# Projections and feed-forward: the form of the matmuls chosen group by group, in a new order of instructions

## The chip, the cores and the metric

The program runs on one core of a Trainium2 chip. The metric is the device time of one execution in microseconds; of the kernel before there are three, from 1133.86 to 1136.08, with a median of 1133.97. TensorE appears in the profile as PE (matmuls) and PEld (loads of weights into the array), VectorE as DVE, ScalarE as ACT, GpSimd as POOL, and SyncE, which only starts DMAs, as SP.

## The reference

One block of a transformer with modulation. x has 2048 tokens of width 1024; 32 heads of width 32 share one key and value head; the feed-forward width is 3584. All in bf16.

```
mod = (silu(c) @ w_mod) as six rows: sa, ca, ga, sb, cb, gb
h = layernorm(x) * (1 + ca) + sa
q = h @ wq  (32 heads of 32);  k = h @ wk;  v = h @ wv   (one head)
p = softmax(q k^T / sqrt(32));  o = p v
x = x + ga * (o @ wo)
h = layernorm(x) * (1 + cb) + sb
x = x + gb * ((silu(h @ w1) * (h @ w3)) @ w2)
```

## The kernel before

**Tiling.** Queries go in 8 blocks of 256 tokens (n = 0 to 7), a block in 8 units of 4 heads (f), a unit in 8 steps of 256 keys (j). That makes 512 score steps. One step (`s_exp`) is 8 matmuls of 32 rows, four heads side by side in the array, into four PSUM banks out of the six of tile S6, and two exponentials of 128x1024 on ACT, which write U. The banks form three slots of two; the scores of an exponential wait until the one three before it has read its slot. U is summed in pairs on DVE (PS) and multiplied by V in a column form (`av_mm`, 128x32, four heads beside each other), and the row sums come from products of PS with ONES, also in columns.

**What fills TensorE between score steps.** While ACT works through the exponentials of one block, PE does other products: the q projections (`q_proj`), the output projection of an earlier block (`wo`), its first feed-forward products (`slab`, 14 for a block: 256 columns of w1 and of w3, then a tanh on ACT and two products on DVE), and its second ones (`quarter`, 4 for a block: 28 products for each of two tiles of tokens). In the last block nothing is left for ACT after the last exponential, and the rest of `wo`, `slab` and `quarter` follows on PE alone. The weights of a slab (W13, 512 KB for each of w1 and w3) go round in few buffers, those of a quarter (W2S, 1792 KB) in two; SP starts each load when the last reader of its buffer is done. In the profile and the lists of instructions the feed-forward weights are called W or HT and W2S (some lie in buffers that had other names), the second norm's output and the queries both QT, the gated product HT.

**Two forms.** A product of 128x128 weights can be one matmul (the full form), or four of 128x32 weights, one for each 32 columns of the array (the column form). The `av` products are of the column form anyway. `prods` (lines 890 to 899) writes both versions; `mode_of` (line 533) chooses. For a node with a column version:

```
return n.col[1][0] or ("C" if self.mode in ("A", "C") and self.ncol < self.COLS and self.load < self.FULL else "F")
```

`self.mode` is the form of the matmul before on PE (A stands for av, C for columns, F for full, S for scores), `ncol` counts column nodes since the last av, and `load` is a running count that grows with dense instructions. A node is a group of two products. `n.col[1]` is a list `form` with one entry; in `q_proj`, `wo` and `slab` four nodes, which add up in one bank, share one list, so the first of the four decides for all. The nodes of `quarter` have no column version.

**The order.** Every instruction is a node of a graph (class `Graph`); class `Placer` places nodes on engines. `ORDER` is a long string of node numbers (with a "b" where the second engine that could do it is taken), and the nodes are issued in that order. Each engine works off its own list strictly in order, waiting on semaphores where a node needs another's result. All instructions are issued in line 22 (`play`), so the profile names no other line. A second program with a guard against overflow stands behind a branch and is not executed here.

Of the kernel before, what the change touches and what calls it, by code (L numbers as in the profile page):

```python
# [8 lines left out]
P = 128  # L9
# [110 lines left out]
6 1 11 0 4 2 5 8 3 7 9 12 13 10 25 16-18 59 22 15 14 60 19 61 28 21 62 412 63 27 20 23 64 24 65 26 29 68 30 31 36 45  # L120
37 32 66 33 38 69 39 40 103 67 34 102 41 35 70 104 131 105 71 123 42 72 132 73 122 106 74 43 124 112 107 46 125 44
133 75 126 47 48 134 108 49 135 50 76 136 111 109 127 113 77 137 128b 114 110b 115 129 116 130 117b 78 118 79 80 119
99 172 81 82 171 97 55b 54 53 51 85 58 98b 57 52b 56 173 163 83 86b 174 162 175 138 84 164 182 87 176 139 88 165 89
143 90 166 91 92 142 167 93 94 168 95 183 140 96 144 460 152 145 141b 120 146 151 461 169 153 147 121 462 154 148b
463 155 170b 464 149 156 184 242 185 157b 150 186 177b 421 191 465 187 158 243 192 178 159 193 188b 466 194 179b 195
467 160 202 196 468 197b 469 180 161 470 203 198 181 471 204 472 199b 205 189 473 206 211 100 190b 207 474 475 101
208b 227 477 228 212 229 230 200 476 231 213 244 214 209 215 201b 245 478 246 210 216 232 233 247 234 235 217b 479
222 236 223 248 224 225 480 218 249 226 481 219 250 252 253 251 254 255 487 482 257-260 483 256 501 261 220 502 485
237 503 504 221 238 488 239 505 240 262 263 506 241 484 507 491-493 489 494 508 264 265 509 495 510 266 496 497 511
486 498 499 267 268 512 500 513 490 269 514 270 526 307 515 516 308 517 271 309 310 525 518 519 272 520 311 273 274  # L130
528 521 522 275 523 527 302 303 524 276 562 304 563 305 529-531 564 565 306 532 533 566 541 538 539 567 277 540 568
542 534 543 569 535-537 544 278 570 548 571 553 545 572 546 552 279 547 280 573 549 574 550 297 281 575 298 551 299
# [4 lines left out]
640 646-648 661 649 652 650 662 357 663 680 358 359 664 651 665 360 681 666 327 361 328 667 653 668 654 332 669 333  # L137
682 334 670 335 655 671 336 329 672 330 683 322 673 331 674 323 675 684 324 325 676 677 326 337 678 338 685 413 679
703 414 430 339 418 704 417 415 340 416 686 688 705 706 689 690 707 687 691-693 341 694 708 695 709 699 696 710 697
# [8 lines left out]
834 835 930 836 931 1313 840 1314 828 837 1315 457 411 838 1316 839 1317 458 841 1318 842 843 846-848 1319 459 1320  # L148
# [3 lines left out]
911-913 1369 1335 914 915 1370 916 1336 917 918 890 1383 919 972 891 892 1371 1372 893 920 894 895 1373 896 1340 897  # L152
921 951 922 1338 898 1375 1374 923 899 924-926 1341 1376 927 928 900 1342 973 901 1377 902 1378 1386 903 904 1379
905 906 929 907 1380 952 1406 908 1351 1408 1381 932-934 1407 935 936 1352 937 938 1387 939 1392 940 993 1354 1393
1384 1409 1394 1355 1410 1395 1396 941 1397 1398 1411 1399 1356 1412 1388 942 1413 943-945 1402 946 1414 947 1389
1415 948 1382 949 1416 953 1390 994 954-956 1417 950 1418 957 1385 958 1419 959 960 844 1432 963 1014 964 961 965
1421 1420 966 962 967 968 1433 969 1422 970 974 1391 1015 975 976 1423 971 1424 977 978 845 1425 979 1435 980 981
984 982 1035 985 1427 1426 1436 986 987 983 988 989 1428 990 991 995 992 1036 996 1429 997 1455 1400 1456 998 1401
999 1000 1430 1001 1457 1002 1016 1056 1017 1458 1437 1003 1018 1019 1459 1020-1022 1004 1023 1460 1461 1431 1077
1441 1442 1024 1403 1443 1434 1444 1462 1445 1025 1446-1448 1404 1463 1464 1438 1005 1006 1465 1007 1405 1008 1439  # L160
1009 1010 1466 1011 1451 1467 1440 1012 1468 1026 1481 1057 1027-1030 1469 1470 1013 1031 1032 1471 1482 1033 1037
1078 1038 1034 1039 1472 1040 1473 1041 1474 1042 1484 1043 1044 1047 1045 1098 1048 1476 1475 1485 1049-1051 1046
1052 1477 1053 1054 1058 1055 1099 1059 1478 1060 1504 1449 1505 1061 1450 1062 1063 1479 1064 1506 1065 1507 1119
1490 1452 1491 1066 1492 1453 1493 1508 1494 1067 1495 1496 1454 1497 1509 1510 1500 1068 1486 1069 1511 1070-1073
1512 1074 1487 1513 1075 1488 1514 1079 1120 1080 1081 1076 1082 1083 1515 1480 1516 1084 1085 1517 1483 1086 1089
1140 1090 1489 1091 1087 1092 1519 1518 1088 1093-1095 1530 1520 1096 1100 1141 1101 1102 1521 1103 1097 1522 1104
1531 1105 1523 1106 1107 1533 1110 1161 1111 1108 1525 1524 1112 1109 1113-1115 1534 1526 1116 1117 1121 1118 1162
1122 1527 1123 1553 1498 1124 1554 1499 1125-1127 1501 1128 1555 1502 1556 1738 1503 1539 1540 1129 1528 1541 1542
1557 1543-1545 1130 1546 1558 1559 1549 1131 1529 1132 1560 1133 1134 1532 1135 1136 1561 1535 1562 1137 1138 1563
1142 1739 1143 1139 1144 1145 1564 1536 1565 1146 1147 1537 1566 1148 1149 1579 1152 1759 1153 1150 1154 1155 1567  # L170
1568 1151 1156 1157 1538 1158 1569 1159 1163 1160 1760 1164 1165 1570 1571 1580 1547 1166 1572 1548 1167-1169 1550
1170 1551 1573 1574 1780 1552 1173 1174 1577 1171 1175 1176 1575 1177-1179 1172 1180 1576 1781 1600 1181 1183 1184
1601 1578 1185-1187 1583 1188 1602 1603 1585 1586 1604 1581 1587-1590 1605 1606 1582 1591 1592 1607 1189 1596 1190
1584 1191 1192 1608 1609 1593 1594 1610 1193 1595 1194-1196 1611 1597 1598 1612 1197 1624 1198 1613 1199-1202 1614
1599 1615 1625 1203 1204 1616 1626 1205-1208 1617 1209 1618 1627 1210 1619 1214 1211 1244 1215-1217 1620 1212 1621
1628 1218 1219 1622 1220-1223 1629 1623 1647 1224 1225 1648 1226 1630 1227 1632 1633 1649 1650 1631 1634 1635 1651
1636-1639 1652 1653 1643 1228 1229 1654 1230 1231 1640 1641 1655 1671 1656 1232 1233 1657 1234 1235 1672 1236 1237
# [229 lines left out]
7223 7264-7270 7273 7271 7274-7276 7272 7277 7289 7278-7288 7290  # L407
# [1271 lines left out]
```

## Time and profile before

| | us |
|---|---|
| median of three executions | 1133.97 |
| the profiled execution's span | 1132.8 |
| start to the first exponential | 30.95 |
| first to the end of the last exponential | 1001.55 |
| end of the last exponential to the end | 100.30 |

The profiled execution's own span is 1132.8; some 1.2 us of the median lie outside it. The profile page gives busy times of each engine. A row of the groups names the engine, the operation, the tile written and those read, the shape and the count, then busy time and mean duration of one, then the idle time ahead of them and what ended it. A row of the timeline has the start, the time to the end of the last of the instructions merged into it, and in brackets the idle time ahead of it with what it waited for. "128*32" behind a matmul is the size of its weights in the array; in the lists of instructions the same reads "32x256", that is 32 columns out and 256 wide. A matmul's own duration (273 ns) is longer than its share of PE's time, since matmuls overlap; the time from start to start counts.

### The profile page before, as it was taken

The numbers are of one execution on the slowest core, as the hardware profiler recorded it, in microseconds if no ns is written. First come the engines' busy times: TensorE is split into PE (matmuls) and PEld (weight loads), VectorE is DVE, ScalarE is ACT, GpSimd is POOL, SyncE is SP. The second block draws the span as 40 slices with busy tenths as digits, with TensorE's granted clock in tenths as the row PEclk, the third lists the DMA queues.
The fourth block names the chain that finished last, engine by engine and source line by source line (L and its number), as shares of the span: only waits on it lengthen the run. The fifth ranks groups of instructions, "written<-read, shape, count | busy, mean of one in ns | idle before, by whom it ended". The sixth has DMA issues, their size and how long they took to land.

```text
span 1132.8 us, 36935 instructions
## 1 busy us (share of the span) xinstructions
PE 1104.8 (98%) x16642; PEld 754.1 (67%) x16642; DVE 983.7 (87%) x1615; ACT 1021.8 (90%) x1160; POOL 41.0 (4%) x92
## 2 busy tenths in 40 slices
PE   6999999999999999999999999999999999999998
PEld 5744546766567766777577766776567756776887
DVE  7998999897889889998999899998999999997442
ACT  5999999999999999999999999999999999994110
POOL 4300000000000000000000000000000010000000
PEclk9999999999999999999999999999999999999999
DMA  9321487664476675965496577868597557777893
GB/s 345 108 76 32 155 217 202 197 191 110 123 224 196 174 195 150 247 193 154 122 290 197 144 190 193 236 196 217 141 253 215 160 148 194 219 204 196 235 240 105
DMA packets 379429, 209.16 MB, mean 185 GB/s; under 512 B 15488, under 2 KB 371072, under 8 KB 379264
## 3 DMA queue, kind: packets, MB, share of 16 engines
q1 hardware_dynamic: 378832, 206.59, 65.8%
q8 instruction: 132, 2.16, 0.8%
q14 instruction: 33, 0.27, 0.1%
q10 hardware_dynamic: 432, 0.13, 0.0%
HBM read 199.89 MB, written 4.19 MB: 180 GB/s over the span
## 4 chain that ended last, share of the span: by engine, by line
ACT 46%; PE 43%; DVE 6%; DMA 3%; issue 1%; SPq 1%; POOL 0%; DVEq 0%
ACT U L22 44%; PE PB L22 31%; PE S L22 13%; ACT HT L22 3%; DVE PS L22 2%; DMA W<-in_A_wq_dram 1%; DVE ST L22 1%; DMA W2S<-in_B_w_dram 1%; DVE HT L22 1%; SPq L22 1%; DMA W<-in_B_w_dram 1%; DVE X L22 0%; POOL RS L22 0%; DVE QT L22 0%; DVE RB L22 0%
## 5 line engine op out<-in xcount | busy, mean ns | idle before, releaser
L22 ACT ACTIVATE U<-S 128x1024 bf16<-128x1024 f32 x1024 | 967.5, 1143 | 5.3 <-PE S L22 3.9
L22 DVE TENSOR_TENSOR PS<-U 128x2048 bf16<-128x2048 bf16 x256 | 309.1, 1213 | 16.6 <-ACT U L22 14.8
L22 DVE TENSOR_TENSOR PS<-PS 128x1024 bf16<-128x1024 bf16 (+1 forms) x401 | 272.4, 690 | 4.2
L22 PE MATMUL PB<-QT,W 128*128 128x256 bf16 (+1 forms) x2448 | 228.4, 273 | 0.6 <-DVE QT L22 0.5
L22 PE MATMUL S<-QT,KT 32*128 32x256 bf16 x4096 | 203.7, 273 | 7.4 <-ACT U L22 4.7
L22 PEld LDWEIGHTS PB<-QT,W 128*128 128x128 bf16 (+1 forms) x2448 | 169.3, 97 | 43.5 <-issue 22.8
L22 PE MATMUL PB<-W2S,HT 128*128 128x256 bf16 x1512 | 190.2, 273 | 0.0
L22 PEld LDWEIGHTS PB<-W2S,HT 128*128 128x128 bf16 x1512 | 136.9, 98 | 42.2 <-issue 24.0
L22 PEld LDWEIGHTS S<-QT,KT 32*128 32x128 bf16 x4096 | 60.9, 92 | 135.2 <-ACT U L22 115.3
L22 PE MATMUL PB<-U,V 128*32 128x256 bf16 x4096 | 128.7, 273 | 0.6 <-ACT U L22 0.5
L22 PE MATMUL PB<-QT,HT 128*128 128x256 bf16 (+1 forms) x1248 | 116.5, 273 | 1.2 <-issue 1.1
L22 PEld LDWEIGHTS PB<-U,V 128*32 128x32 bf16 x4096 | 101.4, 96 | 23.1 <-issue 13.3
L22 PE MATMUL PB<-HT,W 128*32 128x512 bf16 (+2 forms) x800 | 100.0, 338 | 0.9 <-DVE HT L22 0.9
L22 PEld LDWEIGHTS PB<-QT,HT 128*128 128x128 bf16 (+1 forms) x1248 | 85.1, 97 | 22.0 <-issue 11.7
L22 ACT ACTIVATE HT<-PB 128x512 bf16<-128x512 f32 (+1 forms) x106 | 79.5, 750 | 3.6 <-PE PB L22 3.4
L22 DVE SCALAR_TENSOR_TENSOR HT<-HT,PB 128x512 bf16<-128x512 bf16 x99 | 67.6, 683 | 7.4 <-ACT HT L22 6.3
L22 DVE TENSOR_TENSOR HT<-HT,PB 128x512 bf16<-128x512 bf16 x100 | 68.2, 683 | 5.5 <-PE PB L22 4.4
L22 PEld LDWEIGHTS PB<-HT,W 128*128 128x128 bf16 (+1 forms) x800 | 50.1, 97 | 32.9 <-issue 11.5
L22 ACT ACTIVATE HT<-S 128x512 bf16<-128x512 f32 (+1 forms) x17 | 11.8, 696 | 61.6 <-PE S L22 61.6
L22 PE MATMUL PB<-WO,QT 128*128 128x512 bf16 x224 | 55.7, 381 | 0.0
L22 DVE STREAM_TRANSPOSE RB<-PB 128x256 f32<-128x256 f32 x63 | 28.0, 445 | 25.6 <-PE PB L22 25.5
L22 POOL TENSOR_SCALAR RS<-MV 128x1 f32<-128x1 f32 x32 | 12.3, 387 | 1002.3 <-DVE MV L22 774.8
(119 smaller groups left out, 680.9 us busy)
## 6 DMA issues: line engine op xcount, KB each, us to landing
W<-in_B_w_dram SPq DMA_DIRECT2D x150, 512.0 KB, 4.9
W2S<-in_B_w_dram SPq DMA_DIRECT2D x30, 1792.0 KB, 8.4
HT<-in_B_w_dram SPq DMA_DIRECT2D x74, 512.0 KB, 4.8
W2S<-in_w_mod_dram SPq DMA_DIRECT2D x8, 1024.0 KB, 6.4
X<-in_A_x_dram SPq DMA_DIRECT2D x8, 512.0 KB, 6.7
U<-in_w_mod_dram SPq DMA_DIRECT2D x4, 1024.0 KB, 12.1
out_dram<-X SPq DMA_DIRECT2D x7, 512.0 KB, 8.2
W2S<-in_A_x_dram SPq DMA_DIRECT2D x5, 512.0 KB, 12.2
```

The costliest lines, as they stand in the source:

```text
L22: return getattr(e, call[0])(*call[1], **call[2])
```

## The change

Four edits of the code and a new table.

- In `q_proj`, `wo` and `slab` each node has its own list `[None]` in place of the shared `form`. Each group of two products takes the form that PE's state suggests when its turn comes, and one bank can be summed in both forms.
- In `quarter` the nodes are built with `prods` and so have a column version.
- The full version passes skip_group_check=True, as the column version did.
- `SWITCH`, the placer's cost for a change of form, is 0.096 and 0.121 for F and S, where it was 0.095 and 0.11.
- `ORDER` is another order of the same nodes.

```diff
 ORDER = """
-6 1 11 0 4 2 5 8 3 7 9 12 13 10 25 16-18 59 22 15 14 60 19 61 28 21 62 412 63 27 20 23 64 24 65 26 29 68 30 31 36 45
...
+11 6 7 5 8 12 9 13 10 16-18 22 15 14 19 21 20 60 59 69 61 68 23 27-29 70 112 24 102 111 113 26 37 36 103 104 123 122
...
 """
...
-    SWITCH = {"F": 0.095, "S": 0.11, "A": 0.106, "C": 0.106}
+    SWITCH = {"F": 0.096, "S": 0.121, "A": 0.106, "C": 0.106}
...
     def prods(lst):
         def full(b=None):
-            return [lambda e, o=o, w=w, x=x, st=st, sp=sp: e.matmul(o(b, 0, P), w(0, P), x(), start=st, stop=sp)
+            return [lambda e, o=o, w=w, x=x, st=st, sp=sp: e.matmul(o(b, 0, P), w(0, P), x(), start=st, stop=sp, skip_group_check=True)
                     for o, w, x, st, sp in lst]
...
             for m in range(2):
                 for sub in range(2):
-                    form = [None]
                     for c0 in range(0, NC, 2):
...
-                           vt=vt + 0.01 * m, mode="F", sess=ss[m], post=0.145, col=(cols, form))
+                           vt=vt + 0.01 * m, mode="F", sess=ss[m], post=0.145, col=(cols, [None]))
...
                 for f0 in range(0, NF, 2):
-                    op("pe", lambda b, t=t, f0=f0: [lambda e, f=f: e.matmul(
-                        BANK[b][:, t * B:(t + 1) * B], HHT[:, f, t * P:(t + 1) * P], w2[:, f, :], start=(f == 0),
-                        stop=(f == NF - 1)) for f in range(f0, f0 + 2)], pe_mm(B, 2),
-                       reads=[key] + [("HHT", x) for x in range(f0 // 2, (f0 + 1) // 2 + 1)],
-                       writes=[("f2", n, q, t), ("f2", n, q)], vt=vt, mode="F", sess=s, post=0.145)
+                    full, cols = prods([(
+                        lambda b, y, z, t=t: BANK[b][y:z, t * B:(t + 1) * B],
+                        lambda y, z, t=t, f=f: HHT[:, f, t * P + y:t * P + z],
+                        lambda f=f: w2[:, f, :], f == 0, f == NF - 1) for f in range(f0, f0 + 2)])
+                    op("pe", full, pe_mm(B, 2), reads=[key] + [("HHT", x) for x in range(f0 // 2, (f0 + 1) // 2 + 1)],
+                       writes=[("f2", n, q, t), ("f2", n, q)], vt=vt, mode="F", sess=s, post=0.145, col=(cols, [None]))
```

The edit of `form` in `q_proj` and `wo` reads as in `slab`. What the new order does is seen in the lists of instructions. Three places of PE's list follow; `S<-QT,KT` is a score step, `PB<-QT,W` and `PB<-QT,HT` are slab products, `PB<-W2S,HT` quarter products, `PB<-U,V` av products, and `PS,ONES` the row sums.

Near the end of the third block's scores, at 382 us of the profile. Before:

```order
L22 MATMUL PB<-QT,HT 128x256 x14
L22 MATMUL S<-QT,KT 128x256 x8
L22 MATMUL PB<-QT,HT 128x256 x8
L22 MATMUL PB<-QT,W 128x256 x8
L22 MATMUL S<-QT,KT 128x256 x8
L22 MATMUL PB<-PS,ONES 32x256 x4
L22 MATMUL PB<-QT,W 32x256 x96
L22 MATMUL S<-QT,KT 128x256 x8
L22 MATMUL PB<-W2S,HT 128x256 x12
```

Of the change:

```order
L22 MATMUL PB<-QT,HT 128x256 x4
L22 MATMUL PB<-QT,W 128x256 x8
L22 MATMUL S<-QT,KT 128x256 x8
L22 MATMUL PB<-PS,ONES 32x256 x4
L22 MATMUL PB<-QT,W 32x256 x64
L22 MATMUL S<-QT,KT 128x256 x8
L22 MATMUL PB<-QT,W 128x256 x8
L22 MATMUL PB<-W2S,HT 128x256 x4
L22 MATMUL S<-QT,KT 128x256 x8
L22 MATMUL PB<-W2S,HT 128x256 x14
L22 MATMUL S<-QT,KT 128x256 x8
```

The slab products that stood in one run of 96 column matmuls between two score steps stand on both sides of a score step now, 64 in columns and 8 in full form.

The end of the loop, the last two score steps and what comes behind them. Before:

```order
L22 MATMUL PB<-W2S,HT 128x256 x22
L22 MATMUL S<-QT,KT 128x256 x8
L22 MATMUL PB<-W2S,HT 128x256 x12
L22 MATMUL S<-QT,KT 128x256 x8
L22 MATMUL PB<-W2S,HT 128x256 x22
L22 MATMUL PB<-U,V 32x256 x64
L22 MATMUL S<-W2S,HT 128x256 x12
```

Of the change:

```order
L22 MATMUL PB<-W2S,HT 128x256 x12
L22 MATMUL S<-QT,KT 128x256 x8
L22 MATMUL PB<-W2S,HT 128x256 x14
L22 MATMUL S<-QT,KT 128x256 x8
L22 MATMUL PB<-W2S,HT 128x256 x28
L22 MATMUL S<-U,V 32x256 x8
L22 MATMUL PB<-W2S,HT 32x256 x16
L22 MATMUL S<-U,V 32x256 x8
L22 MATMUL PB<-W2S,HT 32x256 x16
L22 MATMUL S<-U,V 32x256 x48
```

The step of 22 products ahead of the second but last score step has 12; behind the last score step stand more quarter products, some of them in columns between the av products.

The slabs of the last block, behind the last exponential. Before:

```order
L22 MATMUL S<-QT,W 128x256 x16
L22 MATMUL S<-QT,HT 128x256 x16
L22 MATMUL PB<-QT,W 128x256 x2
L22 MATMUL S<-QT,W 128x256 x12
L22 MATMUL PB<-QT,W 128x256 x6
L22 MATMUL S<-QT,W 128x256 x16
L22 MATMUL PB<-QT,W 128x256 x4
```

Of the change:

```order
L22 MATMUL S<-QT,W 128x256 x36
L22 MATMUL PB<-QT,W 128x256 x2
L22 MATMUL S<-QT,HT 128x256 x2
L22 MATMUL PB<-QT,W 128x256 x4
L22 MATMUL S<-QT,HT 128x256 x4
L22 MATMUL PB<-QT,W 128x256 x6
L22 MATMUL S<-QT,HT 128x256 x2
L22 MATMUL PB<-QT,W 128x256 x2
L22 MATMUL S<-QT,HT 128x256 x10
```

Before, a buffer of weights is mostly read by 16 matmuls in a row; now the groups of two that use different buffers alternate, so the last reader of a buffer comes later and the next load into it starts later.

More of the change, by code (lines that the diff above doesn't have):

```diff
@@ new lines @@
+1739 1780 1244 1620 1624 1595 1626 1211 1597 1628 1621 1214 1215 1622 1216-1219 1647 1623 1648 1649 1220-1222
+1632-1634 1650 1635 1636 1223 1637 1224 1651 1652 1638 1653 1225 1639 1226-1228 1598 1627 1630 1625 1212 1631 1599
+1643 1629 1654 1656 1640 1229 1641 1230-1232 1655 1642 1644 1645 1657-1659 1245 1246 1233-1235 1247 1660-1664
+1248-1251 1236-1238 1665 1252-1256 1239 1666 1668 1257 1258 1667 1669 1670 1240 1259 1260 1241 2158 1261 2159 1673
+1671 1675 1646 1672 1676 1242 1677 1674 1678 2160 1262 1263 1679-1681 2161 1682 1264 1683 1684 2162 1685 1265 2164
@@ new lines @@
+2063 1823 1822 1843 1790 2301 2303 2304 2291 2292 2278 1305 1791 2248 2249 2295 2281 2282 1803 1804 2305 1805
+1792-1795 2306 2307 1796 2308 1806 1797-1799 1807 2309 2283 2284 1800 2310 1808 1809 2311 1810 1813 1814 2312 1811
+2313 2325 1812 1815-1818 2314 1819 1820 2315 1824-1826 1821 2316 1827 2317 2293 1828 1829 2318 1830 2294 1831
+1834-1837 2320 1838 1832 2319 1844 1885 1864 1865 2296 2328 1833 2321 1839-1841 1845 1846 2348 1847 1848 2323 1842
+2329 2322 2349 2350 1849-1851 2334 1852 2351 2335 2336 1853 2337 2352 2338-2340 2353 2341 2354-2356 2297 2326 2330
@@ new lines @@
+2000 2008 2460 2472 2001 2431 2462 2009 2013 2014 2010 2015 2463 2016 2464 2440 2017 2465 2018 2441 2019-2021
+2023-2026 2467 2027-2030 2475 2022 2473 2476 2443 2470 2031 2033 2466 2468 2034 2495 2035 2036 2469 2496 2497
+2037-2041 2498 2481 2042 2482 2043 2483 2484 2499-2501 2485 2502 2486 2044 2487 2045 2488 2504 2046-2050 2503 2477
+2471 2474 2478 2444 2479 2445 2480 2491 2505 2506 2051 2507 2489 2052-2055 2508 2490 2056 2057 2510 2064 2065
+2058-2060 2066 2509 2521 2061 2631 2094 2511-2513 2067-2071 2514 2072 2073 2516 2074-2076 2515 2077 2517 2078 2079
@@ new lines @@
+3288-3290 3305 2829 3291 3306 3292 3277 3250 3251 2830 3293-3295 2831 3308 3307 3278 3252 3298 3284 3281 3285 3309
+3310 2832-2837 3311 2842-2845 2838 2846 3312 2839 3286 3313 2847 3314 2848 2849 2852 2853 3315 2850 3328 2851
+2854-2857 3317 2858 3316 3318 3319 2859 2863 2864 3287 2860 2865 2866 3320 3296 2867 2868 3329 3297 2869 2870 3321
+2871 2873-2876 3323 2877-2880 3326 2872 3327 3299 3331 2881 2883 3322 3324 3325 2884 3351 2885 2886 3352 3353
+2887-2891 3354 3337-3340 2892 3341 3355-3357 2893 3358 2894-2898 3360 3342 3343 2899 3344 2900 2901 3359 3300 3333
@@ new lines @@
+4410-4412 4893 4862 4413 4918 4414 4406 4426 4427 4448 4468 4447 4415 4919 4902-4905 4920 4906 4891 4864 4416 4907
+4921 4908 4909 4417 4922 4923 4865 4894 4866 4912 4892 4924 4418-4423 4925 4428 4424 4429-4432 4895 4425 4898
+4926-4928 4438 4433-4435 4929 4436 4439-4443 4931 4899 4437 4930 4932 4933 4444 4445 4449-4452 4934 4453 4935 4942
+4446 4897 4900 4943 4454-4456 4459-4461 4937 4462 4463 4457 4458 4901 4936 4938 4464-4466 4470 4471 4467 4945 4489
+3006 4510 4469 4490 4472 4965 4910 4473-4475 4939 4966 4967 4911 4476 4477 4968 4951 4952 4478 4953 4954 4969
@@ new lines @@
+4955-4957 4970 4958 4971 4940 4913 4256 4479 4914 4941 4915 4961 4946-4948 4491 4492 4972 4973 4493-4496 4974 4480
+4481 4497 4498 4482 4975 4499 4500 4483-4486 4977 4487 4501-4504 4944 4949 4488 4950 4976 4978 4979 4505 4980
+4506-4508 4512-4514 4981 4509 4982 4983 4959 4515-4517 4960 4991 4962 4518 4531 4511 4552 3007 4553 4532 4984 4519
+4522-4524 4986 4525 4526 4985 4520 4987 4527-4529 4988 4963 4521 4964 4530 4989 4992 4994 4533 5014 4534 5015
+4535-4540 5017 5000-5002 5016 4541 5003 5018 5004 5005 4542 5019 5006 5007 5020 5021 4543-4548 5023 4549 5022 4550
@@ new lines @@
+5149 5148 5151 5669 5155 5150 5153 5154 5681 4714 4715 5682 5158-5160 4716 5654 5649 5651 5161 5162 5683 5684
+5163-5166 5685 5179 5180 5686 5181 5167 5182-5184 5687 5185 5186 5189 5688 5190 5187 5191 5689 5192 5193 5690 5656
+4717 5652 5188 5194 5195 5691-5693 5196 5168-5173 5694 5174 5695 5175 5657 5699 5197 5658 5700 5176 5200 5696
+5201-5203 5722 5667 5204 5205 5668 5723 5206 5207 5708-5710 5725 5711 5724 5208 5219 5240 5220 5261 5241 5450 5726
+5712 5713 5670 5697 5671 5209 5714 5715 5727 5210 5728 5729 5698 5672 5718 5702 5211-5216 5731 5221 5217 5222-5225
@@ new lines @@
+6210 6192 6193 6685 6194 6195 6211 6656 6196 6686 6197 6687 6198 6212-6214 6688 6657 6199 6658 6689 6215-6217
+6690-6692 6218 6219 6223-6226 6693 6227 6220 6228 6694 6229 6230 6233 6231 6695 6659 5968 6660 6701 6232 6702
+6234-6236 6696 6237 6238 6697 6239 6240 6244-6246 6724 6241 6704 6698 6669 6247-6249 6725 6726 6670 6250 6251 6727
+6710 6711 6243 6263 4719 6284 6285 6264 6336 6252 6712 6713 6728 6714 6699 6672 6253 6715-6717 6265 6730 6266 6729
+6731 6732 6673 6674 6720 6700 6706 6707 6267-6272 6254 6733 6255 6273 6256 6734 6274 6257 6258 6735 6259-6261 6736
@@ new lines @@
+7120-7124 7115 7116 7125 7104-7108 6427 7117 7141 7142 7126 7143 7127 7144 7145 7130-7132 7146 7133 7134 7147 7148
+7135 7151 7152 7136 7137 7153-7158 7149 7128 7192 7129 6428 7150 7138 7159 7161-7182 7193 7183 7184 7194 7185 7195
+7196 7186 7187 7197-7199 7188 7200-7202 7189 7190 7203 7225 7204 7226 7205 7206 7227 7228 7207 7229-7235 7208
+7236-7240 7209 7241 7210 7211 7242 7212-7214 7243 7244 7215-7222 7257-7261 7245 7246 7262 7263 7247 7264-7267 7248
+7268-7270 7249 7250 7273-7275 7251 7252 7276-7286 7271 7253 7254 7272 7287 7288 7191 6429 7223 7255 7289 7290
@@ L1138, in q_proj @@
                 op("pe", full, pe_mm(w, 2) * cold, reads=wk + hk, writes=[("q", n, f)], vt=vt, mode="F", sess=s, post=0.145,
-                   col=(cols, form))
+                   col=(cols, [None]))
             op("dve", lambda b: [lambda e: e.tensor_scalar(
@@ L1386, in wo @@
                     s = Sess()
-                    form = [None]
                     for q in range(4):
@@ L1395, in wo @@
                            reads=[(k, *i) for f in range(2 * q, 2 * q + 2) for k, i in (("QT", (n, f)), ("WOG", (f,)))],
-                           writes=[("wo", n, t, h)], vt=vt, mode="F", sess=s, post=0.145, col=(cols, form))
+                           writes=[("wo", n, t, h)], vt=vt, mode="F", sess=s, post=0.145, col=(cols, [None]))
                     xs = X1[:, n % NX, t, h * 512:(h + 1) * 512]
@@ L1462, in slab @@
                 for sub in range(2):
-                    form = [None]
                     for c0 in range(0, NC, 2):
```

464 lines of the change are left out of this document (220 added, 244 removed), and 43 rows, old and new, of the table ORDER.

## The prediction

> **What bounds the kernel now.** I read the page's busy shares first, then the windows, cut at the first and the last exponential, then the timeline of ScalarE and TensorE at the places where ScalarE stands idle.
>
> ```profile
> span 1132.8 us, 36935 instructions
> PE 1104.8 (98%) x16642; PEld 754.1 (67%) x16642; DVE 983.7 (87%) x1615; ACT 1021.8 (90%) x1160; POOL 41.0 (4%) x92
> ...
> 0.00:30.95 30.95, 19.73 (x287) 16.79 (x288) 23.50 (x59) 18.07 (x20) 14.72 (x43) 1.00 0.99 346
> 30.95:1032.50 1001.55, 988.67 (x15454) 654.99 (x15453) 917.95 (x1479) 995.40 (x1128) 24.47 (x46) 1.00 0.65 178
> 1032.50:1132.80 100.30, 96.39 (x906) 82.33 (x903) 42.27 (x78) 8.38 (x15) 1.76 (x4) 1.00 0.76 202
> ```
>
> The columns of the last three rows are the stretch, its length, the busy time of PE, weight loads, DVE, ACT and POOL, the granted clock and the DMA share. There are three parts: 30.95 us of startup, a body of 1001.55 us in which ACT is busy for 995.40, and a tail of 100.30 us in which only PE is full. The clock is 1.00 in all three, so it plays no part.
>
> In the body ACT sets the end: it has only 1001.55 - 995.40 = 6.15 us of idle time. PE is nearly as full, but waits for ACT to free the banks of the scores:
>
> ```profile
> PEld S L22 <- ACT U L22: 115.3, 413, 1.1
> ...
> ACT U L22 <- PE S L22: 3.9, 9, 0.9
> ...
> 54.02 112.61 ACT L22 ACTIVATE U<-S 128x1024 bf16<-128x1024 f32 x122 [0.40 <-PE PB L22]
> ...
> 385.92 0.72 ACT L22 ACTIVATE HT<-PB 128x512 bf16<-128x512 f32 x1
> 386.42 1.15 ACT L22 ACTIVATE U<-S 128x1024 bf16<-128x1024 f32 x1
> 388.10 4.69 ACT L22 ACTIVATE U<-S 128x1024 bf16<-128x1024 f32 x5 [0.54 <-PE S L22]
> ```
>
> 122 exponentials took 112.61 us, or 0.92 each; a tanh pushes the next one back by 386.42 - 385.92 = 0.50. One score step feeds two exponentials, so PE has 1.84 us from step to step, 2.34 with a tanh. The last row shows a break: ACT stood for 0.54 us because a score step came late; the waits (first two rows: total, times, longest) count nine such, 3.9 us together. What PE did ahead of it:
>
> ```profile
> 384.38 0.40 PE L22 MATMUL S<-QT,KT 32*128 32x256 bf16 x8
> 384.70 0.29 PE L22 MATMUL PB<-PS,ONES 128*32 128x256 bf16 x4
> 384.82 2.79 PE L22 MATMUL PB<-QT,W 128*32 128x256 bf16 x96
> 387.55 0.51 PE L22 MATMUL S<-QT,KT 32*128 32x256 bf16 x8
> ```
>
> The step took 387.55 - 384.38 = 3.17 us, 0.83 over 2.34. PE's lead over ACT took 0.29 of that and ACT lost 0.54. I call "unit" one product of 128x128 by 128x256, either one matmul in the full form or four in the column form. This step holds 24 + 1 units and 2 for the scores; 27 units in 3.17 us, less two changes of form, leave 0.109 us a unit if a change costs 0.11.
>
> **The change part by part.** What the form itself costs:
>
> ```profile
> 54.14 1.04 PE L22 MATMUL PB<-HT,W 128*128 128x512 bf16 x4
> 55.11 0.40 PE L22 MATMUL S<-QT,KT 32*128 32x256 bf16 x8
> ...
> 56.34 1.04 PE L22 MATMUL PB<-HT,W 128*32 128x512 bf16 x16
> 57.30 0.40 PE L22 MATMUL S<-QT,KT 32*128 32x256 bf16 x8
> ...
> L22 PEld LDWEIGHTS PB<-QT,W 128*128 128x128 bf16 x1584 | 144.3, 98 | 41.7 <-issue 21.7 <-DVE QT L22 1.4 <-DVE PS L22 0.4
> L22 PEld LDWEIGHTS PB<-QT,W 128*32 128x32 bf16 x832 | 21.8, 97 | 1.4 <-issue 1.1
> ```
>
> Eight units took 55.11 - 54.14 = 0.97 us in full form and 57.30 - 56.34 = 0.96 in columns, each with one change behind it. So the form is free; only the change of form costs. The 1579 matmuls more (counted in the two built programs: 16642 and 18221) are whole units turned into four pieces, and weigh nothing by these rows. The Trainium skill, "TensorEngine Tiling (Array Packing)", section Restrictions, speaks against that: column tiling switches Fast Weight Load off. The rows above do not bear it out as a loss here: 97 against 98 ns a load, and the same step time. By that rule the sum below would only grow.
>
> *Changes of form.* Counted in the two instruction lists they fall from 1109 to 1059; 50 x 0.11 = 5.5 us less work for PE, all in the body. This by itself gains nothing, since ACT ends the body; it counts only where a step overruns.
>
> *Body.* With 0.109 a unit and 0.1 a change I added up each of the 511 stretches from score step to score step in both lists. Before, 201 exceed ACT's 1.84 (2.34), by 50.6 us together; after, 174 by 32.6. The deepest are gone: four steps of 27 units (the one at 384.38 and its three like in other blocks) and one of 24 near the end:
>
> ```profile
> 513.01 1.94 ACT L22 ACTIVATE U<-S 128x1024 bf16<-128x1024 f32 x2 [0.51 <-PE S L22]
> ...
> 763.64 1.94 ACT L22 ACTIVATE U<-S 128x1024 bf16<-128x1024 f32 x2 [0.50 <-PE S L22]
> ...
> 889.03 1.94 ACT L22 ACTIVATE U<-S 128x1024 bf16<-128x1024 f32 x2 [0.47 <-PE S L22]
> ...
> 1028.74 3.77 ACT L22 ACTIVATE U<-S 128x1024 bf16<-128x1024 f32 x4 [0.90 <-PE S L22]
> ...
> 1025.79 2.57 PE L22 MATMUL PB<-W2S,HT 128*128 128x256 bf16 x22
> 1028.30 0.40 PE L22 MATMUL S<-QT,KT 32*128 32x256 bf16 x8
> ```
>
> In the new order the same place holds 64 column matmuls, a score step, then the rest in full form: 16 + 1 + 2 units and two changes, 2.3 us, within 2.34. The idle time that goes is 0.54 + 0.51 + 0.50 + 0.47 + 0.90 = 2.92 us; a break also costs up to 0.22 more, because an exponential alone takes 1.15 (row 386.42) and one in a row 0.92. Five breaks are worth 2.92 to 4.0; I take 3.5. Against it, three new steps exceed by about 0.71 (26 units with a tanh): 0.71 - 0.29 = 0.42 each, +1.3 (bounds 0 and +1.9). The shallow overruns that are left shrink by a third, from 46.3 us to 30.5. Of ACT's idle time 3.9 - 2.92 = 0.98 us is put down to them by name, at most 6.15 - 2.92 = 3.23 with all that names nothing: -0.3 to -1.1, and I take -0.7. Body: -3.5 + 1.3 - 0.7 = **-2.9** (bounds -4.0 - 1.1 = -5.1 and -2.9 + 1.9 = -1.0).
>
> *Tail, work.* Behind the last score step PE has 895 units before and 909 after (the instruction lists): 14 x 0.109 = **+1.5**. This is the price of the relief in the body: what no longer overruns there is done later, where nothing hides it.
>
> *Tail, loads.* PE waited for two loads before:
>
> ```profile
> 1030.04 0.40 PE L22 MATMUL S<-QT,KT 32*128 32x256 bf16 x8
> ...
> 1035.39 1.48 PE L22 MATMUL S<-W2S,HT 128*128 128x256 bf16 x12 [0.58 <-DMA W2S<-in_B_w_dram]
> ...
> 1082.18 1.48 PE L22 MATMUL S<-QT,W 128*128 128x256 bf16 x12 [0.48 <-DMA W<-in_B_w_dram]
> ...
> W<-in_B_w_dram SPq DMA_DIRECT2D x150, 512.0 KB, 4.9
> W2S<-in_B_w_dram SPq DMA_DIRECT2D x30, 1792.0 KB, 8.4
> ```
>
> A weight buffer is loaded again when its last reader has ended. From there to the first matmul that reads the new contents I counted units of PE. Before, the shortest distance in the tail was 5.7 us (the second wait: 5.7 + 0.48 = 6.2 needed), the others 6.5 or more. After, five buffers have 4.8, 4.8, 5.0, 5.0 and 5.0, four more 5.4 to 5.9. The median landing is 4.9, the one late load 6.2: I take 5.3, which waits 2 x 0.5 + 3 x 0.3 = 1.9. For W2S the distance grows from 8.6 (0.58 short, so 9.2 needed) to 9.6: 0.3 for the queue. Sum 2.2 against 0.58 + 0.48 = 1.06: **+1.1** (bounds: at 4.9, 0.2 - 1.06 = -0.9; at 5.7, 4.4 + 0.8 - 1.06 = +4.1).
>
> *Startup.* The first exponential hangs on eight scalings of the first wq columns and on the projection behind them:
>
> ```profile
> 24.37 1.71 DVE L22 TENSOR_SCALAR WO<-W,MODC 128x256 bf16<-128x256 bf16 x6 [0.40 <-DMA W<-in_A_wq_dram]
> ...
> 24.43 2.03 POOL L22 TENSOR_SCALAR WO<-W,MODC 128x256 bf16<-128x256 bf16 x2 [1.10 <-DMA W<-in_A_wq_dram]
> ...
> 27.46 1.05 PE L22 MATMUL PB<-HT,WO 128*128 128x256 bf16 x8 [0.84 <-POOL RS L22]
> ...
> 28.63 1.91 PE L22 MATMUL PB<-HT,WO 128*128 128x256 bf16 x16
> 30.47 0.40 PE L22 MATMUL S<-QT,KT 32*128 32x256 bf16 x8
> ```
>
> In the new lists POOL does three of them, up to 24.43 + 3 x 1.0 = 27.5, about when PE's first bank came free before, and the 24 matmuls run with no warm-up products among them: 2.6 us in place of 3.0, of which a later start takes part. I take -0.1, with 0.5 either way (half a scaling on POOL). SP's queue holds the same bytes ahead of wq. The end of the program, two DVE operations and the last output, is as it was: nothing.
>
> *Sum:* -0.1 - 2.9 + 1.5 + 1.1 = -0.4. The profiled span of 1132.8 becomes 1132.4. The median of the runs, 1133.97, is 1.2 above that span, so the median should be 1133.6.
>
> **The rivals.**
>
> *Faster: the body wins and the loads arrive.* Body -4.6, near its lower bound, and tail waits as before: -0.1 - 4.6 + 1.5 + 0 = -3.2, 1130.8. For it: 413 waits of PE on ACT mean that PE has room in most steps. Against it: the tail must have +1.5, and distances of 4.8 leave nothing.
>
> *Slower: the tail's loads.* Place: PE's slab matmuls behind the last score step. If a 512 KB load needs 5.7 us from release to landing there, as the one at 1082.18 needed more, the loads cost +4.1 and with a body of -2.0 the sum is -0.1 - 2.0 + 1.5 + 4.1 = +3.5, 1137.5. With the body at -2.9 the loads turn the sign from +1.5 on (a landing of about 5.4) and can be told from no change from +3.8 on (about 5.65). For it: DMA is busy at 0.76 of the tail and a wait pushes only PE. Against: before, all but one of the loads came in time.
>
> *Slower: PE runs out of instructions.* PE stood still twice in the body with no semaphore named, 1.1 us together:
>
> ```profile
> PE PB L22 <- issue: 1.1, 2, 0.9
> ...
> q8 instruction: 132, 2.16, 0.8%
> ```
>
> Fetching came in 132 packets. Stretches of 128 matmuls issued in under 4.3 us number 103 in the list before and 635 after; if such gaps grew by the same factor, 1.1 would become 6.8, and with +5.7 on top of the sum the time is 1139.3. Against: the densest stretch is no denser (3.69 us before, 3.79 after). The Trainium skill, "Runtime: NRT & Kernel Launch", section Instruction fetch mechanics, says that fetching runs ahead in order and is hidden by issue; by it this rival costs nothing, and the 1.1 is something else. No run here settles it.
>
> *The change does nothing* is excluded: the new list has 1632 column matmuls in the second feed-forward product, where there were none.
>
> **How the numbers follow.** A measurement of this kernel tells about 0.2%, 2.3 us, from no change. My forecast, body gain given back in the tail, ends within that: chance 0.35, by itself 1131.7 to 1136.2. The faster case has 0.32; the two slower ones 0.23 and 0.10, together 0.33. The range takes the low bound (-0.5 - 5.1 + 1.5 - 0.9 = -5.0, 1129.0) and on the other side the loads at 4.1 with the body at its worst, -0.1 - 1.0 + 1.5 + 4.1 = +4.5, 1138.5; some of the fetch case reaches beyond, so 1128.7 to 1139.5.
>
> **What would show it.** The windows of the new profile, cut at its first and last exponential: a body about 3 us shorter with ACT idle for 3 to 4 us in it; no [.. <-PE S] of 0.5 at the four places; a tail of 102 to 104 us; in its waits five or more on W in place of one, and their sum against 1.06. Forecast wrong on the fast side: tail waits near 1 us. Wrong on the slow side: waits on W above 4 us, or PE gaps put down to issue that sum to more than 3 us.

## The result and the profile after

The change made the kernel slower: 1144.53 us, the median of four executions (1143.45 to 1146.27), against 1134.87 for the kernel before in four executions on the same chip (1133.86 to 1136.08). The ratio is 1.0086, with a 95% interval from 1.0074 to 1.0099. The forecast was 1133.6 with a range up to 1139.5, so the time lies outside it.

The page of the changed kernel, its opening rows and two of its queues and groups; behind them the windows, cut at its first and its last exponential, with the columns of the prediction's:

```profile
span 1142.2 us, 40103 instructions
PE 1105.3 (97%) x18221; PEld 756.8 (66%) x18221; DVE 969.2 (85%) x1616; ACT 1019.6 (89%) x1158; POOL 43.8 (4%) x93
...
q8 instruction: 145, 2.38, 0.9%
...
L22 ACT ACTIVATE U<-S 128x1024 bf16<-128x1024 f32 x1024 | 966.1, 1145 | 11.0 <-PE S L22 10.1
```

```profile
0.00:31.26 31.26, 18.79 (x246) 15.44 (x247) 23.81 (x60) 15.95 (x17) 15.02 (x43) 0.95 0.97 346
31.26:1039.40 1008.14, 988.16 (x17019) 658.01 (x17019) 903.83 (x1477) 995.80 (x1128) 27.23 (x47) 1.00 0.67 176
1039.40:1142.20 102.80, 98.36 (x961) 83.36 (x958) 41.57 (x80) 7.82 (x14) 1.57 (x4) 1.00 0.78 208
```

The span grew by 1142.2 - 1132.8 = 9.4 us: +0.3 in the startup, 1008.14 - 1001.55 = +6.6 in the body, 102.80 - 100.30 = +2.5 in the tail. No engine has much more to do: PE is busy for 1105.3 us against 1104.8, and ACT in the body for 995.80 against 995.40. What grew is ACT's idle time there, 12.34 us against 6.15. The waits of the changed kernel say whom ACT waits for, and whom PE (total, times, longest):

```profile
ACT U L22 <- PE S L22: 10.1, 16, 2.8
...
PE PB L22 <- issue: 5.1, 4, 2.2
...
PE S L22 <- issue: 2.3, 3, 0.9
PE S L22 <- DMA HT<-in_B_w_dram: 1.0, 3, 0.6
```

ACT waited for scores 10.1 us instead of 3.9, and PE stood for 5.1 + 2.3 = 7.4 us in seven places where no semaphore is named, instead of 1.1 in two. An eighth gap, of 1.32 us, is of the same kind, as will be seen. The largest of them, in PE's timeline and then in ACT's:

```profile
881.49 1.71 PE L22 MATMUL PB<-U,V 128*32 128x256 bf16 x56
883.15 0.40 PE L22 MATMUL S<-QT,KT 32*128 32x256 bf16 x8
...
885.12 0.40 PE L22 MATMUL S<-QT,KT 32*128 32x256 bf16 x8
885.45 0.39 PE L22 MATMUL PB<-QT,W 128*128 128x256 bf16 x2
888.07 1.84 PE L22 MATMUL PB<-QT,W 128*128 128x256 bf16 x10 [2.24 <-issue]
889.85 0.61 PE L22 MATMUL S<-QT,KT 32*128 32x256 bf16 x8
```

```profile
881.94 5.73 ACT L22 ACTIVATE U<-S 128x1024 bf16<-128x1024 f32 x6
890.51 1.02 ACT L22 ACTIVATE U<-S 128x1024 bf16<-128x1024 f32 x1 [2.84 <-PE S L22]
892.25 0.60 ACT L22 ACTIVATE HT<-PB 128x512 bf16<-128x512 f32 x1 [0.72 <-PE PB L22]
```

PE breaks off two matmuls into a run of twelve that use the same tiles, and stands for 2.24 us; the score step behind it comes at 889.85, and ACT has been without work for 2.84 us. The transfers before PE ran dry, and from there until it went on (two windows of the DMA view: packets, MB, share of 16 engines):

```profile
DMA packets 2235, 1.13 MB, mean 290 GB/s; under 512 B 24, under 2 KB 2235, under 8 KB 2235
...
q1 hardware_dynamic: 2235, 1.13, 119.2%
...
q1 hardware_dynamic: 1533, 0.78, 115.5%
q8 instruction: 1, 0.02, 2.8%
```

From 881.5 to 885.4 the packets of weights (q1) come to more than the whole time of all 16 DMA engines, and no packet of the instruction queue q8 ran. From 885.4 to 888.1 one did, which started at 885.49; PE went on 2.58 us later.

All such gaps stand at like places. The q8 packets hold 2.38 MB / 145 = 16 KB each. Between the two kernels they grew by 13 and the page's instructions by 40103 - 36935 = 3168, so a packet holds some 244. Counting PE's list (a weight load and a matmul make two, a wait one), I found each of the eight gaps at a place that leaves 190 or 191 when divided by 256. So does the larger gap of before (the other one there, of 0.23 us, leaves 185 and is not of this kind), in PE's timeline of before:

```profile
315.90 0.39 PE L22 MATMUL PB<-QT,HT 128*128 128x256 bf16 x2
317.16 1.03 PE L22 MATMUL PB<-QT,HT 128*128 128x256 bf16 x8 [0.86 <-issue]
```

The eight gaps of after and this one of before, worked out from the timeline, the list and the q8 packets. The list is cut into blocks of 256; "takes" is PE's time for the block ahead of the gap, "fetch" is how long after that block's first instruction the q8 packet for the next one started:

```
 gap at    stood   block takes   fetch starts after
 212.12    0.93       5.41            3.65
 242.56    1.14       5.19            3.67
 379.42    0.84       5.67            3.79
 507.29    1.17       4.76            3.09
 541.75    0.56       5.35            3.18
 633.67    1.32       4.64            3.51
 888.07    2.24       4.35            4.00
1043.93    0.49       6.16            4.07
before:
 317.16    0.86       4.71            3.07
```

Read the row of 888.07: PE entered the block at 881.49 and had worked it off 4.35 us later; the fetch of the next one had been held up for 4.00 us, and about 2.6 us pass from its start to the first new matmul, so PE stood for 4.00 + 2.6 - 4.35 = 2.25. (At 633.67 the profile names a DVE operation as the releaser; it had ended 0.51 us earlier.) A gap needs two things at once: a block that PE works off quickly, and a fetch that starts so late that its delay and the 2.6 us together are longer than PE's time for the block. Blocks of under 5.7 us whose fetch starts over 2.4 us late are found 3 times before and 9 times after; the gap at 1043.93 is not among them, since its block took 6.16 us and its fetch was 4.07 us late. A fetch starts about 0.3 us (median) after PE enters a block where the DMA engines are under 0.1 busy in the next microsecond, and 2.2 to 2.4 us, up to 6.4, where they are over 0.9 busy.

The clock has a part in the price of the largest gap. From 888.65 to 892.00 the granted clock of PE is 0.50, and matmuls start 0.21 us apart in place of 0.11, so PE stays late after it has its instructions back. Over the whole execution the mean granted clock of the changed kernel is 0.993 to 0.996, against 0.997 to 1.000 in 17 executions of the kernel before, so the clock is a rival, too.

### The profile page after: what moved, and what is told of

The parts are those of the page before. It is cut to its first block, busy times and chain, and to the rows that moved or that the text cites. A ratio compares the mean times of both kernels' runs of the same rounds, so it can differ in the third digit from the quotient of the medians.

```text
span 1142.2 us, 40103 instructions
## 1 busy us (share of the span) xinstructions
PE 1105.3 (97%) x18221; PEld 756.8 (66%) x18221; DVE 969.2 (85%) x1616; ACT 1019.6 (89%) x1158; POOL 43.8 (4%) x93
## 3 DMA queue, kind: packets, MB, share of 16 engines
q8 instruction: 145, 2.38, 0.9%
## 4 chain that ended last, share of the span: by engine, by line
PE 53%; ACT 35%; DVE 5%; DMA 4%; issue 1%; POOL 1%; SPq 1%; DVEq 0%; POOLq 0%
PE PB L22 39%; ACT U L22 33%; PE S L22 13%; ACT HT L22 2%; DVE PS L22 2%; DMA HT<-in_B_w_dram 1%; DMA W<-in_A_wq_dram 1%; DMA W2S<-in_B_w_dram 1%; POOL RS L22 1%; SPq L22 1%; DVE ST L22 1%; DMA W2S<-in_w_mod_dram 1%; DVE QT L22 1%; DVE X L22 0%; DVE XNB L22 0%
## 5 line engine op out<-in xcount | busy, mean ns | idle before, releaser
L22 ACT ACTIVATE U<-S 128x1024 bf16<-128x1024 f32 x1024 | 966.1, 1145 | 11.0 <-PE S L22 10.1
L22 DVE TENSOR_TENSOR PS<-PS 128x1024 bf16<-128x1024 bf16 (+1 forms) x401 | 268.0, 687 | 1.9
L22 PE MATMUL PB<-QT,W 128*128 128x256 bf16 (+1 forms) x2650 | 238.0, 274 | 4.0 <-issue 3.4
L22 PE MATMUL PB<-W2S,HT 128*32 128x256 bf16 (+1 forms) x2724 | 201.7, 273 | 1.3 <-DMA W2S<-in_B_w_dram 0.6
L22 PEld LDWEIGHTS PB<-W2S,HT 128*32 128x32 bf16 (+1 forms) x2724 | 144.0, 97 | 34.4 <-issue 19.7
L22 PE MATMUL PB<-U,V 128*32 128x256 bf16 x4032 | 141.4, 274 | 0.7 <-DVE RB L22 0.4
L22 PE MATMUL PB<-QT,HT 128*128 128x256 bf16 (+1 forms) x1388 | 129.3, 273 | 1.3 <-DVE PS L22 1.3
L22 PEld LDWEIGHTS PB<-U,V 128*32 128x32 bf16 x4032 | 97.2, 96 | 29.6 <-issue 18.1
L22 PEld LDWEIGHTS PB<-QT,HT 128*128 128x128 bf16 (+1 forms) x1388 | 90.6, 97 | 23.0 <-issue 10.9
L22 PE MATMUL PB<-HT,W 128*128 128x256 bf16 (+3 forms) x722 | 102.6, 331 | 0.8 <-DVE HT L22 0.8
L22 PE MATMUL PB<-WO,QT 128*128 128x512 bf16 (+1 forms) x286 | 58.8, 380 | 0.0
```

The costliest lines, as they stand in the source:

```text
L22: return getattr(e, call[0])(*call[1], **call[2])
```

## The experiments

Theory F: PE runs out of instructions, where column matmuls stand close and weight loads hold the fetch up. The rivals: the forms themselves cost something, the new order is worse by its steps alone, the tail's loads do it, PE simply has too many instructions, or PE's clock does it.

**e1_forms: the new forms with the old order.** The changed code (groups that choose for themselves, quarters in columns) with the table of before:

```diff
 ORDER = """
-11 6 7 5 8 12 9 13 10 16-18 22 15 14 19 21 20 60 59 69 61 68 23 27-29 70 112 24 102 111 113 26 37 36 103 104 123 122
+6 1 11 0 4 2 5 8 3 7 9 12 13 10 25 16-18 59 22 15 14 60 19 61 28 21 62 412 63 27 20 23 64 24 65 26 29 68 30 31 36 45
...
```

> The order of before with the new code (each group of two chooses its form, quarter products may be columns). Theory F: the 9.7 us come from PE running out of instructions: 16 KB blocks of 256 instructions that PE works off in under 5.5 us while the next block's fetch waits behind weight loads. Here few blocks are that short (17542 matmuls in place of 18221), so PE gaps without a semaphore sum to 1 to 3 us and the time is 1134 to 1137. Rival C, the free choice of form itself costs (columns are dearer than they look): most of the loss is here too, 1141 or more.

Measured: 1134.39 us (10 executions), ratio 1.0000 [0.9988, 1.0013]. Its windows, and its gaps in the waits:

```profile
31.02:1033.80 1002.78, 987.11 (x16318) 659.39 (x16317) 918.58 (x1479) 995.52 (x1128) 24.42 (x46) 1.00 0.65 178
1033.80:1132.70 98.90, 96.09 (x942) 82.58 (x939) 42.26 (x78) 8.38 (x15) 1.76 (x4) 1.00 0.78 205
```

```profile
PE PB L22 <- issue: 0.7, 1, 0.7
PE S L22 <- issue: 0.4, 1, 0.4
```

17542 matmuls, 900 more than before, at the same time, with 1.1 us of gaps. In the old order the code's edit is harmless.

**e2_order: the new order with the old forms.** The changed table with the code of before (shared `form`, quarters only in full form, the old `SWITCH`).

```diff
-                           vt=vt + 0.01 * m, mode="F", sess=ss[m], post=0.145, col=(cols, [None]))
+                           vt=vt + 0.01 * m, mode="F", sess=ss[m], post=0.145, col=(cols, form))
...
```

> The new order with the old code (one form for four groups, quarter products in full form only). 1269 changes of form in place of 1059 and 17105 matmuls. Theory F: short blocks remain in some places, gaps of 4 to 7 us, and the 210 changes more overrun many score steps, some 9 us: 1147 to 1153. Rival O, the order is harmless and the loss is all in the forms: 1134 to 1137.

Measured: 1155.84 us (4 executions), ratio 1.0184 [1.0153, 1.0215]. It has 17105 matmuls, and its gaps at borders are 4.33 us in five, fewer than after. PE is busy for longer:

```profile
PE 1122.0 (97%) x17105; PEld 739.3 (64%) x17105; DVE 970.5 (84%) x1616; ACT 1025.7 (89%) x1158; POOL 45.0 (4%) x93
```

Its list has 1269 changes of form, 210 more than after; at the prediction's 0.11 us they are 23 us of PE's time, against 1122.0 - 1105.3 = 16.7 more that it is busy. So this run loses mainly by changes of form, and the new order needs the new forms. But half as much of gaps as after (4.33 against 8.69 us) comes with the new order alone, and the new forms bring it up.

**e3_shift: the block borders moved.** The changed kernel with 96 matmuls of one column each ahead of the first warm-up product. They move everything behind them by 192 places in PE's list.

```diff
+        more = 96 if wait else 0
+
         def _run(eng):
             if wait:
                 eng.wait_ge(sem[need.sem], need.val)
+            for _ in range(more):
+                play(eng, short(REC))
```

> The changed kernel with 96 one-column matmuls put ahead of its first warm-up products, which moves every later PE instruction by 192 places, three quarters of a block. Theory F: the gaps without a semaphore no longer stand at the same eight matmuls but again where the place in PE's list is the same number above a multiple of 256; from the lengths of the new blocks their sum should be some 6 us in place of 8.7, the time 1140 to 1143. Rival C (gaps belong to certain matmuls or bursts of columns): the same matmuls, the same sum, 1144 to 1146.

Measured: 1144.01 us (1138.70 to 1146.34, 4 executions), ratio 1.0088 [1.0071, 1.0105]. The place that lost 2.24 us, with other instructions at its border, in PE's timeline:

```profile
879.51 1.48 PE L22 MATMUL PB<-QT,W 128*32 128x256 bf16 x48
880.93 0.40 PE L22 MATMUL S<-QT,KT 32*128 32x256 bf16 x8
881.25 1.48 PE L22 MATMUL PB<-QT,W 128*128 128x256 bf16 x12
882.67 0.40 PE L22 MATMUL S<-QT,KT 32*128 32x256 bf16 x8
883.00 1.59 PE L22 MATMUL PB<-QT,W 128*128 128x256 bf16 x13
884.92 0.50 PE L22 MATMUL PB<-QT,W 128*128 128x256 bf16 x3 [0.33 <-issue]
```

The twelve matmuls run through. A gap of 0.33 stands 10 + 8 + 13 = 31 matmuls behind the old one, which is 62 places of the list, and the border had moved by 256 - 192 = 64. The other gaps moved too, each to a place that again leaves 190 or 191. That binds them to the place in the list and not to what is computed there. The time is a miss: the profiled execution, with 2.8 us of gaps, was the fastest of the four by 4.4 us, and the median is where it was. The three slower ones have no trace, and their mean granted clock is lower (0.994 to 0.997 against 0.998), so how much they lose at the new borders is not shown.

**e4_loads: the load on the DMA engines taken away.** From the second block of tokens on, each load of w1 and w3 brings one eighth of its bytes, and each of w2 into its two regular buffers one seventh. Every instruction of PE is as in the changed kernel.

```diff
+                few = 1 if n and not guarded else NC
-                dma("sp", W13SL[r][:, m], w[:, s * 256:(s + 1) * 256].rearrange("(c p) f -> p c f", p=P), ("W13", r, m),
+                dma("sp", W13SL[r][:, m, 0:few], w[0:few * P, s * 256:(s + 1) * 256].rearrange("(c p) f -> p c f", p=P), ("W13", r, m),
...
+            few = 4 if n and key[0] == "W2S" and not guarded else NF
```

> The changed kernel with most of the feed-forward weights left out of the loads from the second block of tokens on: an eighth of each w1 or w3 slab and a seventh of each w2 quarter is loaded (the rest stays from earlier loads, so the result is another), all waits and all work on PE as before. Theory F with fetches queued behind loads: each fetch starts within about 0.5 us of the block's beginning, the gaps go (under 1.5 us in the whole body, those of the first block of tokens may stay), the tail's waits on W go too: 1133 to 1136.5. Rival D, density alone (PE outruns a fetch of fixed length): the gaps stay at 7 to 9 us, 1142 or more.

Measured: 1133.57 us (1130.14 to 1137.13, 10 executions), ratio 0.9982 [0.9971, 0.9993], 11 us below the changed kernel. Its body, its one gap, and the same place as above (its profiled execution was the slowest of the ten):

```profile
31.20:1034.80 1003.60, 990.22 (x17019) 658.40 (x17019) 904.48 (x1477) 994.89 (x1128) 27.23 (x47) 0.99 0.22 62
...
PE PB L22 <- issue: 0.8, 1, 0.8
```

```profile
882.90 1.48 PE L22 MATMUL PB<-QT,W 128*32 128x256 bf16 x48
884.32 0.40 PE L22 MATMUL S<-QT,KT 32*128 32x256 bf16 x8
884.64 1.49 PE L22 MATMUL PB<-QT,W 128*128 128x256 bf16 x12
```

The DMA share of the body falls from 0.67 to 0.22, one gap of 0.8 us is left, and it stands in the first block, where the loads are still whole. As many blocks are worked off in under 5.5 us as in the changed kernel (17), but fetches that start over 2.4 us late are 11 instead of some 41. This is the run that parts the theories: the matmuls, their number, their forms and their order are all there, and the loss is not. Nor is it the clock: four of the ten executions have a mean granted clock of 0.994, like the changed kernel's, and took 1132.85 to 1137.13 us, where the changed kernel's fastest took 1143.45. The kernel before was not run with the same loads cut, so what smaller loads would win there is not known. The tail lost its waits on loads too, 1.04 us, which is all that the rival of the tail's loads could claim.

**e5_full18 and e6_full0: fewer columns.** `load` in `mode_of` is the kernel's own count of dense instructions; over `FULL` a group takes the full form. The changed kernel with a lower limit:

```diff
-    FULL = 36.0
+    FULL = 18.0
```

In e6_full0 it is 0.0, so that every group takes the full form.

> The changed kernel with the placer's limit FULL at 18 in place of 36: the same order, but a group goes back to the full form sooner (17561 matmuls in place of 18221, 1122 changes of form in place of 1059). Theory F: fewer short blocks, gaps of 2 to 5 us in place of 8.7, and about 1 us lost to changes of form: 1138 to 1142. Rival C/O (the loss is not in the fetches): gaps and time as the changed kernel or slower, 1144 or more.

> The changed kernel with FULL at 0: the same order, every group in full form (15353 matmuls, 1295 changes of form). Theory F: no block of instructions is short enough, gaps under 0.5 us in all; but 236 changes more than the changed kernel, at 0.11, overrun the score steps by some 10 us: 1143 to 1149. Rival (gaps without a semaphore have nothing to do with columns): gaps of 5 us or more remain.

Measured: e5_full18 1139.48 us (6 executions), ratio 1.0039 [1.0027, 1.0052], with 17561 matmuls and 1122 changes of form. e6_full0 1148.91 us (4 executions), ratio 1.0103 [1.0081, 1.0126], with 15353 matmuls and 1295 changes. Half the limit wins half of the loss back; its profiled execution, the fastest of the six, has gaps of 2.1 us at two borders. With no group in columns no gap at a border is left, but 236 changes of form more than after take the gain and more: the window of its body is longer than after's, with PE busy for 999.48 us in place of 988.16.

```profile
32.50:1044.70 1012.20, 999.48 (x14154) 635.45 (x14193) 905.22 (x1478) 1001.26 (x1128) 27.56 (x46) 1.00 0.66 174
```

**e7_w2only: only the loads of w2 cut.** The second half of e4_loads alone.

> The changed kernel with only the w2 quarters cut (a seventh of each is loaded from the second block of tokens on, except the last two; the rest stays from earlier loads), w1 and w3 whole. In the changed kernel five of the eight gaps had a w2 load under way at the block's beginning, three only w1 and w3. Theory F: gaps of 2 to 5 us, 1137 to 1141. Rival D (fetches are late for another reason): gaps of 7 to 9, 1142 or more.

Measured: 1140.06 us (6 executions), ratio 1.0038 [1.0021, 1.0054]: 4.5 us of the 11. The profiled execution was the slowest of the six. Its six gaps at borders come to 5.2 us, a little over what was expected, and five of them stand at the same matmuls as in the changed kernel; the largest, in PE's timeline:

```profile
888.74 1.27 PE L22 MATMUL PB<-QT,W 128*128 128x256 bf16 x10 [1.29 <-issue]
```

So there are three lengths for one place with one list of instructions: 2.24 us with all loads, 1.29 without most of w2, none without most of w1 and w3 too (one profiled execution each).

**e8_many: no limit on columns in the old order.** e1_forms with both limits (`COLS`, `FULL`) at 1000, so that columns run on where PE is in them.

> The order of before with the new code and no limit on columns (FULL and COLS at 1000): 18328 matmuls, more than the changed kernel has, at 1058 changes of form. Theory F: it is not the number, but short blocks where a fetch is late, and this order has few of them: gaps of 1 to 3.5 us, 1134 to 1138. Rival N (PE has too many instructions as such): gaps as in the changed kernel, 1142 or more.

Measured: 1136.60 us (10 executions), ratio 1.0012 [1.0002, 1.0022]. The expectation had its count wrong. The profile shows 17716 weight loads, one for each matmul (of the matmuls themselves 33 records are missing):

```profile
PE 1098.0 (97%) x17683; PEld 758.8 (67%) x17716; DVE 984.3 (87%) x1615; ACT 1021.4 (90%) x1160; POOL 40.8 (4%) x92
```

That is 174 more than e1_forms and 505 fewer than the changed kernel, so this run does not test rival N as it was meant to. It loses 1.4 us against the kernel before. Its gaps at borders are 1.11 us in the body and one in the tail:

```profile
1043.29 4.07 PE L22 MATMUL S<-WO,QT 128*32 128x512 bf16 x72 [1.92 <-issue]
```

It is e4_loads that answers rival N: with the same 18221 matmuls the loss is gone. What decides is whether dense blocks meet busy DMA engines, and in the old order they seldom do.

## Why the prediction was wrong, step by step

**The step that failed** is "The 1579 matmuls more ... weigh nothing by these rows", and with it the case "PE runs out of instructions". The rows compared the time that eight units take in the two forms, and there the forms are equal; but a unit in columns is eight places of PE's list (four weight loads and four matmuls) in place of two, and the list itself has to be brought in. That case named the right mechanism, priced it at +5.7 and gave it a chance of 0.10. It measured more: ACT's idle time behind the seven gaps of the body is 0.85 + 1.02 + 0.63 + 0.98 + 0.36 + 1.21 + 3.56 = 8.61 us (in the last of them with the half clock's part), and the gap of the tail adds 0.49. The reason for the low price was that gaps would scale from 1.1 us with the number of dense stretches. The reason for the low chance was that "the densest stretch is no denser": true, but density is only one of two conditions. The other, how late the fetch starts, stood in the trace of before (25 fetches over 2.4 us late) and was not looked at. The Trainium skill, "Runtime: NRT & Kernel Launch", section Instruction fetch mechanics, says that the sequencer refills in blocks of 256 instructions and that this is hidden by issue. The trace agrees on the block (16 KB packets, gaps 256 places apart or a multiple of it) and contradicts the second part: 8.7 us of gaps in one execution.

**Body, -2.9.** Right but for the gaps. ACT's idle time in the body is 12.34 us after, of which 8.61 stand behind the gaps at borders; what is left, 3.73, is 2.3 less than before, where 6.15 - 0.14 = 6.01 are left. ACT's work grew by 0.4, so without the gaps the body is some 1.9 us shorter, within the bounds of -5.1 and -1.0. The place that the prediction spoke of, in PE's timeline of after:

```profile
387.27 0.40 PE L22 MATMUL S<-QT,KT 32*128 32x256 bf16 x8
387.59 0.29 PE L22 MATMUL PB<-PS,ONES 128*32 128x256 bf16 x4
387.71 1.92 PE L22 MATMUL PB<-QT,W 128*32 128x256 bf16 x64
389.56 0.40 PE L22 MATMUL S<-QT,KT 32*128 32x256 bf16 x8
```

The step takes 389.56 - 387.27 = 2.29 us, as worked out (2.3), and ACT does not break off there. But such column matmuls are the relief and part of the cause in one: each of the eight blocks ahead of a gap holds 32 to 48 of them beside the av products, which are in columns anyway.

**Tail, work, +1.5.** About right: of +2.5, 0.49 is the gap at 1043.93 and nothing comes from the loads, which leaves 2.0.

**Tail, loads, +1.1.** Wrong in size: 0.

```profile
1073.94 0.61 PE L22 MATMUL S<-QT,HT 128*128 128x256 bf16 x4 [0.26 <-DMA HT<-in_B_w_dram]
...
1086.68 0.61 PE L22 MATMUL S<-QT,HT 128*128 128x256 bf16 x4 [0.56 <-DMA HT<-in_B_w_dram]
...
1106.58 1.27 PE L22 MATMUL S<-QT,HT 128*128 128x256 bf16 x10 [0.22 <-DMA HT<-in_B_w_dram]
```

Three waits of 1.04 us together, against 1.06 before, where five or more were expected. The rival of the tail's loads falls with it. The loads were not fast: the median of the tail's 15 loads named W, from issue to landing, is 5.7 us, at which the prediction's own sum has over 5 us of waits. So the distances from a buffer's last reader to its next, as counted, do not say how long PE waits; why, no run shows. That work (+1.5) and loads (+1.1) gave +2.6 for the tail and +2.5 was measured is luck: the loads gave nothing, and a gap and more work stand in their place.

**Startup, -0.1.** +0.3, within the 0.5 allowed; the granted clock there was 0.95 in place of 1.00, for which the prediction had no term.

**What would show it** held: PE's gaps put down to issue above 3 us were named as the sign of a miss on the slow side, and they came to 7.4. The sign for the fast side, tail waits near 1 us, showed as well, and the tail of 102.80 us lay in the forecast 102 to 104; neither says anything of the gaps, which outweighed both.

*Still open.* The executions of one program differ (e3_shift by 7.6 us, e4_loads by 7.0), and their granted clocks differ too (e4_loads took 1130.14 us at 1.000 and 1137.13 at 0.994); with one trace for each program, what the delays of the fetches have in that is not shown. Nor does a run show why one fetch waits for 0.3 us and another for up to 6 behind the loads. An order in which dense blocks and large loads keep apart was not tried; of the runs here that do all of the reference's work none beat the kernel before.

## What to carry to other kernels

Instructions are data too: splitting a matmul into four makes PE's list four times as long there. Where 256 places of it are worked off in less time than the fetch of the next 256 needs, which waits behind weight loads, PE runs dry at the block's border; here such blocks took 4.35 to 6.16 us. Before pricing such a split at nothing, count PE's places, mark each 256th, and compare the time that PE needs for a block with how late the instruction queue's packets start. A count of instructions or of dense stretches alone says little (e4_loads has the same list as the changed kernel and ran 11 us faster); and when a gap without a semaphore stands in the profile of before, look for its place in the list first.

## What the hardware showed that was not expected

- The next block of 256 PE instructions is, as far as these traces show, asked for about when PE enters the block before it (in the changed kernel the packet starts up to 1.6 us earlier in a few blocks, and later in all others), so the lead is one block. From the start of the packet to the first new matmul 2.45 to 2.85 us passed, though the packet itself took about 1.2.
- A packet of instructions starts later when weight loads fill the DMA engines: 0.3 us (median) after PE enters the block with nearly idle DMA engines, 2.2 to 2.4 and up to 6.4 with busy ones. In e4_loads, with a DMA share of 0.22, the median over all fetches was 0.47 in place of 1.25.
- A gap of 2.24 us on PE cost ACT 2.84 + 0.72 = 3.56 us of standing. From 0.5 us after the gap on, the granted clock was 0.50 for 3.4 us: the last ten of the twelve matmuls took 889.85 - 888.07 = 1.78 us up to the next score step, where all twelve took 882.67 - 881.25 = 1.42 in e3_shift, and the tanh behind that step came late too.
